# A fused attention and FFN kernel whose instructions the tile framework orders with its timeline model

## The chip, the cores and the metric

The kernel runs on one core of one Trainium2 chip. The metric is the device time of one execution in microseconds (us), as the median of three runs. Five engines work side by side, each through its own queue of instructions in order: TensorE (PE in the profile; its weight loads are PEld), VectorE (DVE), ScalarE (ACT), GpSimd (POOL) and SyncE (SP, which issues most of the DMA transfers).

## The reference

The reference has two parts. The first is linear attention with random features on q, k and v of 8 batches × 8 heads × 576 tokens × 64, with 128 features per head:

```python
def phi(x):
    proj = np.einsum('bhsd,md->bhsm', x, omega)
    sq = np.sum(x * x, axis=-1, keepdims=True) / 2.0
    h = proj - sq
    h = h - np.max(h, axis=-1, keepdims=True)
    return np.exp(h) / np.sqrt(m)
q_p, k_p = (phi(q_s), phi(k_s))
kv = np.einsum('bhsm,bhsd->bhmd', k_p, v)
z = np.sum(k_p, axis=2)
num = np.einsum('bhsm,bhmd->bhsd', q_p, kv)
den = np.einsum('bhsm,bhm->bhs', q_p, z)[..., None] + 1e-06
return (num / den).astype(np.float32)
```

The second takes that result as x, 4608 tokens of 512 values, through a bilinear FFN whose weights are given in float64 (`w1`, `w2` 512×1024, `w3` 1024×1024, `w_out` 1024×512):

```python
a = x @ w1
b = x @ w2
h = a * b @ w3
return (h @ w_out).astype(np.float32)
```

## The kernel before, in words

The 4608 tokens are 36 chunks of 128, batch after batch; a batch has four chunks and a half. Products are made from pairs of fp16 numbers: every operand is scaled by a power of two and split into a high and a low half, and each product is three matmuls (`PASSES`: high·high, high·low, low·high). The split is made by `split` (ACT or POOL writes the high half, L142 or L144; DVE the low half, L145).

**Weights.** The float64 words come in 20 blocks of 128×1024. `from_float64` (L462 to L494) has three steps for each: `fetch` issues the DMA on ACT's queue (L472), `magnitude` takes the absolute value of the high words on ACT (L480), and `bits` puts the float32 together with four instructions on DVE (L486, L488, L489, L490). `w1` and `w2` go to `w12b`, with sums of magnitudes for the scale (L510 on ACT, L514 on PE), and are split (`w12_split`). `w3` and `w_out` are multiplied once into one matrix: its row blocks are `wp_n` (L560, L562 on PE), which ACT copies to `Wb` (L574) and measures (L159); `W_split` splits them at the end.

**Chunks.** For a chunk of q or k, `norm` and `scale` find a scale from sums of squares, `split` makes `qhl` or `khl`, and `features` projects them on PE (L267, tiles `qpj`, `kpj`), takes the negated maximum on DVE (`nm`, L277), makes the exponential on ACT (L288, or with DVE's L290 first, L291), and splits it (`eq`, `ek`, L131, L133, L300). `kv_batch` forms a batch's `kv` (L348, `kvp`). `eq` is transposed by DMA (`eqT`), and `q_attend` multiplies it with `kv` (L384, `nu`), divides (`gd`, `gr`, `xs`, L394 to L400) and takes a maximum (L407). `x_turn` splits the result (`xhl`, L422 on ACT, L423 on DVE) and transposes it by DMA (`xT`, L427). `gate` makes both products with w1 and w2 (L622, `ab`), multiplies them (ACT L631, DVE L632, `asb`) and splits the result on POOL (L636, L637). `project_out` multiplies with the folded matrix (L651, `o`), scales on ACT (L655) and writes the chunk out. Names carry the chunk's number: `xhl_0` is chunk 0's, `ab_0_0` and `asb_0_0` are the gate of chunk 0, first half of the features. K runs ahead of q by five chunks, so that `kpj_6` goes with `qpj_1`.

**What sets the order.** The source issues the steps by a plan: `step` and `put` give each a tick and a rank, and a loop over the ticks calls them, with weight steps (`ORDER`, `PER`) and pieces of gate and projection between them. The recorded program then goes to the tile framework, which may reorder it: each engine's queue gets its final order from the framework's scheduler, with due regard to what depends on what; `tc.high_priority()` around a step (`x_turn` has it) gives its instructions precedence there. The framework also places the semaphores. Which scheduler is used is set where the context is opened, in `kernel()`, L847.

## Time and profile before

| what | value |
|---|---|
| time, median of three runs | 872.07 us (871.26 to 872.96) |
| profiled execution, first to last instruction | 870.8 us (the profile gives its time as this span alone) |
| mean granted TensorE clock | 0.957 |
| instructions | 20594 |
| busy: PE, DVE, ACT, POOL | 787.7, 614.1, 416.9, 305.4 us |
| moved by DMA | 88.43 MB, mean 102 GB/s |

Busy time is the union of an engine's instructions over the span. The page also cuts the span into 40 slices, 21.8 us each, with a digit for the busy tenths of each engine. A row of the timeline gives start, length, engine, line, operation and tiles, and in brackets the idle time just before with what ended it; a row of the groups gives the busy time of all such instructions in us, the mean of one in ns, and then the idle time before them. [...]

### The profile page before, as it was taken

To read this page: it belongs to the slowest core of one execution; us is meant where nothing else is said; L and a number is where in the kernel's file an instruction comes from. 1 tells how busy PE (TensorE), PEld (TensorE's weight loads), DVE (VectorE), ACT (ScalarE), POOL (GpSimd) and SP (SyncE) were. 2 spreads that over 40 slices of the span, in tenths; PEclk is the share of its full clock that TensorE was granted. 3 is DMA by queue.
4 is the path that set the end of the run, shared out by engine and by line. 5 is a ranking of instruction groups with operands and counts; after the bars stand their busy time and mean duration, and the time that the engine had idled before them with its cause. 6 is when DMAs were issued, how large, how long until landed. Compare 5 with 4: busy or idle time off the path is not lost.

```text
span 870.8 us, 20594 instructions
## 1 busy us (share of the span) xinstructions
PE 787.7 (90%) x8608; PEld 582.9 (67%) x8614; DVE 614.1 (71%) x1116; ACT 416.9 (48%) x748; POOL 305.4 (35%) x327
## 2 busy tenths in 40 slices
PE   0973499568997899999999999999999999999998
PEld 0432355466785777777777777777777767777774
DVE  5879888788868977776877777768777764563200
ACT  3588776777543743545355335453553342221111
POOL 0000003223253654444543544445435452233220
PEclk9985599779998999999999999999999999999999
DMA  8535557332334644434433453334342234332100
GB/s 307 189 109 195 151 150 219 102 82 39 88 96 110 122 89 124 81 87 86 122 98 86 95 125 77 84 86 122 101 90 67 62 78 72 72 62 49 31 19 36
DMA packets 142525, 88.43 MB, mean 102 GB/s; under 512 B 116704, under 2 KB 116832, under 8 KB 142432
## 3 DMA queue, kind: packets, MB, share of 16 engines
q1 hardware_dynamic: 134944, 66.15, 32.5%
q10 hardware_dynamic: 7488, 20.97, 7.1%
q8 instruction: 67, 1.10, 0.5%
q14 instruction: 26, 0.21, 0.1%
HBM read 49.35 MB, written 9.44 MB: 68 GB/s over the span
## 4 chain that ended last, share of the span: by engine, by line
PE 76%; DVE 10%; ACT 6%; DMA 4%; issue 3%; POOL 1%; ACTq 0%; SPq 0%; DVEq 0%; POOLq 0%
PE ab L622 40%; PE o L651 20%; PE kvp L348 3%; PE nu L384 3%; PE wp L562 3%; PE qpj L267 3%; PE kpj L267 2%; DVE nm L277 1%; DVE vhl L145 1%; ACT qe L288 1%; DMA qraw<-qT 1%; ACT ke L288 1%; DVE arena L489 1%; DMA arena<-wo 1%; DVE w12b L490 1%
## 5 line engine op out<-in xcount | busy, mean ns | idle before, releaser
L622 PE MATMUL ab<-xT,w12b 128*128 128x256 f16 (+1 forms) x3840 | 397.9, 264 | 8.4 <-DMA xT<-xhl 6.5
L622 PEld LDWEIGHTS <-w12b 128*128 128x128 f16 x3840 | 344.4, 99 | 50.3 <-issue 8.5
L651 PE MATMUL o<-Wb,arena 128*128 128x512 f16 x864 | 194.1, 379 | 2.2 <-DVE Wb L145 1.4
L651 PEld LDWEIGHTS <-arena 128*128 128x128 f16 x864 | 84.4, 100 | 95.1 <-issue 2.4
L636 POOL TENSOR_SCALAR arena<-asb 128x512 f16<-128x512 f32 x72 | 49.3, 685 | 217.9 <-DVE asb L632 207.3
L300 POOL TENSOR_TENSOR eq<-qe,eq 128x1024 f16<-128x1024 f32 x34 | 73.0, 2148 | 129.1 <-DVE eq L131 90.8
L291 ACT ACTIVATE qe<-qe,ln_e,es 128x1024 f32<-128x1024 f32 x31 | 38.4, 1239 | 112.3 <-DVE qe L290 112.3
L632 DVE TENSOR_TENSOR asb<-ab,asb 128x512 f32<-128x512 f32 x72 | 49.4, 686 | 59.1 <-PE ab L622 57.9
L300 POOL TENSOR_TENSOR ek<-ke,ek 128x1024 f16<-128x1024 f32 x28 | 59.7, 2132 | 88.9 <-ACT ek L133 44.7
L637 POOL TENSOR_TENSOR arena<-asb,arena 128x512 f16<-128x512 f32 x72 | 85.3, 1185 | 5.9
L291 ACT ACTIVATE ke<-ke,ln_e,es 128x1024 f32<-128x1024 f32 x27 | 33.5, 1241 | 79.0 <-DVE ke L290 62.4
L145 DVE SCALAR_TENSOR_TENSOR khl<-kraw,s,khl 128x512 f16<-128x512 f32 x36 | 53.9, 1497 | 16.2 <-ACT khl L142 16.2
L562 PE MATMUL wp<-w12b 128*128 128x512 f32 x128 | 59.0, 613 | 1.4 <-DVE w12b L490 1.4
L145 DVE SCALAR_TENSOR_TENSOR qhl<-qraw,s,qhl 128x512 f16<-128x512 f32 x36 | 32.1, 891 | 37.5 <-ACT qhl L142 37.5
L422 ACT ACTIVATE xhl<-xs,p2r 128x512 f16<-128x512 f32 x36 | 25.9, 719 | 58.1 <-DVE p2r L189 54.4
L631 ACT ACTIVATE asb<-ab 128x512 f32<-128x512 f32 x72 | 41.9, 582 | 24.6 <-PE ab L622 24.6
L267 PE MATMUL kpj<-om,khl 64*128 64x128 f16 x864 | 35.5, 231 | 17.0 <-ACT khl L142 11.5
L159 ACT ACTIVATE junk_q<-qraw 128x512 bf16<-128x512 f32 x36 | 22.7, 630 | 56.5 <-DMA qraw<-qT 56.5
L384 PEld LDWEIGHTS <-eqT 128*128 128x128 f16 (+1 forms) x960 | 32.6, 102 | 24.3 <-DMA eqT<-eq 13.6
L655 ACT ACTIVATE o<-o,oscs 128x512 f32<-128x512 f32 x36 | 24.2, 673 | 50.6 <-PE o L651 50.6
L384 PE MATMUL nu<-kv,eqT 128*128 128x65 f16 (+1 forms) x960 | 34.9, 196 | 13.6 <-DMA eqT<-eq 12.6
L131 DVE CAST eq<-qe 128x1024 f16<-128x1024 f32 x31 | 22.1, 713 | 35.3 <-ACT qe L291 35.3
(124 smaller groups left out, 1053.8 us busy)
## 6 DMA issues: line engine op xcount, KB each, us to landing
kraw<-kT SPq DMA_DIRECT2D x36, 256.0 KB, 2.8
vraw<-v SPq DMA_DIRECT2D x36, 256.0 KB, 3.0
qraw<-qT SPq DMA_DIRECT2D x36, 256.0 KB, 2.8
out<-o SPq DMA_DIRECT2D x36, 256.0 KB, 2.2
arena<-w3T ACTq DMA_DIRECT2D x8, 1024.0 KB, 5.8
arena<-w ACTq DMA_DIRECT2D x8, 1024.0 KB, 5.8
arena<-wo ACTq DMA_DIRECT2D x4, 1024.0 KB, 5.9
eqT<-eq SPq DMA_TRANSPOSE x72, 3.1
```

The lines of the kernel that those rows point to most:

```text
L145: nc.vector.scalar_tensor_tensor(lo, src, s, hi, ALU.mult, ALU.subtract)
L267: nc.tensor.matmul(pg[:, g, i], hl[d, x, i], om[d, y], start=first is None and n == 0, stop=n == len(PASSES) - 1,)
L291: nc.scalar.activation(e, e, AF.Exp, scale=es, bias=ln_e)
L300: (nc.vector if lo == "d" else nc.gpsimd).tensor_tensor(t[:, 1], e, t[:, 0], ALU.subtract)
L384: nc.tensor.matmul(nu[r0:r1, h // 4, h % 4], t[:, x, place(h), r0:r1], kvs[b][:, y, h], start=n == 0, stop=n == 2,)
L562: nc.tensor.matmul(ps, w[:, j, k * P : (k + 1) * P], guest[:, j], start=j == j0, stop=j == HALF - 1,)
L622: nc.tensor.matmul(ps[:, k], w12[m][i][cc][:, a, r * P : (r + 1) * P], x[:, b, cc, off : off + T], start=j == 0, stop=j == len(mm) - 1,)
L631: nc.scalar.mul(asb, ab[0], 2.0**-37)
L632: nc.vector.tensor_tensor(asb, ab[1], asb, ALU.mult)
L636: nc.gpsimd.tensor_scalar(h[:, 0], asb, 1.0, 1.0, ALU.mult, ALU.mult)
L637: nc.gpsimd.tensor_tensor(h[:, 1], asb, h[:, 0], ALU.subtract)
L651: nc.tensor.matmul(ps, hs[c, f][0][:, a], W[f][:, b], start=i == 0, stop=i == len(mm) - 1)
```

## The change

The tile context is opened with one more argument. The scheduler then chooses the order of the instructions with a timeline model of the machine instead of its default rule. Nothing that is computed changes; the matmuls, the passes of each engine and the DMA transfers are the same, in another order within each queue.

```diff
@@ -844,7 +844,7 @@
         for k, a in arrays.items()
     ]
     out = nc.dram_tensor("out", (B * S, arrays["wo"].shape[1]), F32, kind="ExternalOutput").ap()
-    with tile.TileContext(nc) as tc:
+    with tile.TileContext(nc, schedule_with_timeline_sim=True) as tc:
         weights = [a.bitcast(U32) for a in args[4:]]
         tile_favor_attention_then_bilinear_ffn(tc, *args[:4], *weights, out)
     r = run_bass_kernel_spmd(nc, [arrays], core_ids=[0])
```

Three places show what it moves. The numbers in the names below are the framework's own running numbers; what they stand for is said beside each.

DVE, around the low half of x for chunk 0 (`xhl_962` is `xhl_0`; `qhl_925` and `khl_930` are `qhl_1` and `khl_6`; `qpj_967` and `kpj_1010` are `qpj_1` and `kpj_6`). Before:

```order
L419 TENSOR_SCALAR pt_960<-p2p_4_956,pv 128x1
L423 SCALAR_TENSOR_TENSOR xhl_962<-xs_921,p2r_4_958,xhl_962 128x512
L486 TENSOR_SCALAR arena<-arena 128x1024
L145 SCALAR_TENSOR_TENSOR qhl_925<-qraw_496,s_4_880,qhl_925 128x512
L145 SCALAR_TENSOR_TENSOR khl_930<-kraw_528,s_4_880,khl_930 128x512
L488 TENSOR_SCALAR arena<-arena 128x1024
L489 SCALAR_TENSOR_TENSOR arena<-arena 128x1024
L490 SCALAR_TENSOR_TENSOR w12b<-arena 128x1024
L277 TENSOR_REDUCE nm<-qpj_967 128x8
L277 TENSOR_REDUCE nm<-kpj_1010 128x8
L286 TENSOR_SCALAR nm<-nm,es 128x8 x2
```

Now, in the same place:

```order
L394 TENSOR_SCALAR gd<-nu_892 128x8
L398 RECIPROCAL gr<-gd 128x8
L400 TENSOR_TENSOR xs_921<-nu_892,gr 128x512
L277 TENSOR_REDUCE nm<-qpj_967 128x8
L407 TENSOR_REDUCE mx<-xs_921 128x1
L286 TENSOR_SCALAR nm<-nm,es 128x8
L414 TENSOR_SCALAR mx<-mx 128x1
L277 TENSOR_REDUCE nm<-kpj_1010 128x8
L423 SCALAR_TENSOR_TENSOR xhl_962<-xs_921,p2r_4_958,xhl_962 128x512
L131 CAST ek_1047<-ke_1037 128x1024
L300 TENSOR_TENSOR eq_1004<-qe_994,eq_1004 128x1024
```

The two reductions with their two L286 now stand ahead of `xhl_962`, where they stood behind it, and so do the two splits and 18 instructions of weight blocks (five L486, five L488, five L489, three L490), further up in the queue: 24 instructions in all, and none went the other way.

PE, behind the gate matmuls of chunk 0 (`ab_0_1_1129`). `nu_1217` is `nu_1`, the attention product of chunk 1; `norm_q_k_1183` is the norm for q of chunk 2 and k of chunk 7; `wp_0_1199` and `wp_1_1205` are the seventh row block of the folded matrix, `wp_6`; `norm_v_1260` is the norm for v of batch 1. One piece of the difference, without the weight loads:

```order
+L164 MATMUL norm_q_k_1183<-sums_105,ones 128x3
+L560 MATMUL wp_0_1199<-Wb,ident 128x512
+L562 MATMUL wp_0_1199<-w12b 128x512 x4
+L560 MATMUL wp_1_1205<-Wb,ident 128x512
+L562 MATMUL wp_1_1205<-w12b 128x512 x4
 L384 MATMUL nu_1217<-kv_614,eqT_1007 128x65
-L164 MATMUL norm_q_k_1183<-sums_105,ones 128x3
-L560 MATMUL wp_0_1199<-Wb,ident 128x512
-L562 MATMUL wp_0_1199<-w12b 128x512 x4
-L560 MATMUL wp_1_1205<-Wb,ident 128x512
-L562 MATMUL wp_1_1205<-w12b 128x512 x4
 L164 MATMUL norm_v_1260<-vam_866,ones 128x8
```

The ten matmuls of `wp_6` and the norm stood behind the 24 of `nu_1` and now stand ahead of them.

ACT, around the cast of the features of q for chunk 2 (`eq_1341` is `eq_2`; `ke_1374` is k of chunk 7; `asb_0_1511` is the gate of chunk 1). Before:

```order
L288 ACTIVATE qe_1331<-qpj_1304,nm,es 128x128 x8
L288 ACTIVATE ke_1374<-kpj_1347,nm,es 128x128
L133 CAST eq_1341<-qe_1331 128x1024
L288 ACTIVATE ke_1374<-kpj_1347,nm,es 128x128 x7
L631 ACTIVATE asb_0_1511<-ab_0_0_1413 128x512
L133 CAST ek_1384<-ke_1374 128x1024
L510 ACTIVATE wab_2_1_1529<-w12b 128x1024
```

Now:

```order
L288 ACTIVATE qe_1331<-qpj_1304,nm,es 128x128 x8
L480 ACTIVATE arena<-arena 128x1024
L288 ACTIVATE ke_1374<-kpj_1347,nm,es 128x128 x8
L631 ACTIVATE asb_0_1511<-ab_0_0_1413 128x512
L510 ACTIVATE wab_2_1_1529<-w12b 128x1024
L133 CAST eq_1341<-qe_1331 128x1024
L133 CAST ek_1384<-ke_1374 128x1024
```

The cast of `eq_2` moved from behind one exponential of chunk 7 to behind all eight, a magnitude, the scaling of the gate and an L510.

On PE there are further swaps of this kind up to 227 us of the trace and between 268 and 302 us: among them `wp_4` and `wp_5` stand earlier, two matmuls of `nu_3` now stand ahead of `ab_2_0`, and 26 matmuls of `ab_4_2` ahead of `qpj_8`. On SP a few transfers of k change places with outputs.

## The prediction

> **What bounds the kernel now.** I read the page's busy times and its 40 slices first, since a change of order alone can only win or lose idle time.
>
> ```profile
> span 870.8 us, 20594 instructions
> PE 787.7 (90%) x8608; PEld 582.9 (67%) x8614; DVE 614.1 (71%) x1116; ACT 416.9 (48%) x748; POOL 305.4 (35%) x327
> PE   0973499568997899999999999999999999999998
> DVE  5879888788868977776877777768777764563200
> PEclk9985599779998999999999999999999999999999
> ```
>
> A slice is 21.8 us. From the fourteenth on PE stands at nine tenths; the open slices are all at the start, and there DVE is the densest engine and the granted TensorE clock falls to 0.5 and 0.7. The windows view (columns: stretch, length, busy of PE, PEld, DVE, ACT, POOL with their counts, granted clock, DMA share, GB/s) cuts that start where the orders of the two programs part and meet again.
>
> ```profile
> 0.00:20.00 20.00, 1.17 (x4) 1.00 (x4) 10.37 (x28) 6.20 (x10) 1.07 (x16) 1.00 0.90 331
> 20.00:114.00 94.00, 61.16 (x410) 34.23 (x413) 79.82 (x136) 68.59 (x138) 0.67 (x10) 0.75 0.50 160
> 114.00:136.00 22.00, 21.95 (x204) 13.77 (x203) 18.18 (x21) 18.12 (x44) 2.13 (x1) 1.00 0.65 157
> 136.00:156.00 20.00, 16.70 (x86) 7.98 (x85) 18.31 (x36) 10.54 (x22) 6.90 (x7) 1.00 0.68 210
> 156.00:189.00 33.00, 21.08 (x271) 18.84 (x274) 25.88 (x47) 27.25 (x59) 8.09 (x5) 0.69 0.37 89
> 189.00:227.00 38.00, 33.16 (x591) 27.14 (x593) 32.27 (x78) 26.96 (x55) 11.07 (x18) 1.00 0.25 60
> 227.00:270.00 43.00, 43.00 (x540) 33.05 (x535) 34.46 (x52) 16.40 (x25) 22.00 (x19) 1.00 0.37 97
> 270.00:302.00 32.00, 24.52 (x379) 19.73 (x378) 28.32 (x62) 21.41 (x37) 16.24 (x10) 0.89 0.54 108
> 302.00:870.00 568.00, 565.00 (x6139) 427.21 (x6137) 366.50 (x663) 221.43 (x365) 237.19 (x243) 1.00 0.36 81
> ```
>
> Three things follow. From 302 us on PE works 565.0 of 568 us at full clock: with the same matmuls behind it, the end of the program is the moment of 302 us plus 568. All that an order can change lies before that: PE idles there for (20 − 1.2) + (94 − 61.2) + 0.1 + (20 − 16.7) + (33 − 21.1) + (38 − 33.2) + 0 + (32 − 24.5) = 79 us. And from 20 to 227 us DVE is busy for 174.5 of 207 us, more than PE's 154.1: it converts the float64 weights (four instructions to a block, 20 blocks) and also makes each chunk's features, x and splits. So the order on DVE, and what it makes PE wait for, decides the start.
>
> **The change part by part.** Nothing is added or removed, so each cost is a position: how much work of an engine now stands ahead of an instruction on which another engine waits. Up to DVE's reduction `nm` of `qpj_5`, and on PE from the first `o_0` of the projection (both at 227 us of this trace), the two orders hold the same set of work ahead. So I follow one chain from the first place where it is late to 227 us, and add the difference to the end. Its stations before are these (DVE first, then PE; start and length in us).
>
> ```profile
> 113.60 0.75 DVE L423 SCALAR_TENSOR_TENSOR xhl<-xs,p2r,xhl 128x512 f16<-128x512 f32 x1 [0.68 <-ACT xhl L422]
> 115.25 0.75 DVE L145 SCALAR_TENSOR_TENSOR qhl<-qraw,s,qhl 128x512 f16<-128x512 f32 x1
> 115.92 0.75 DVE L145 SCALAR_TENSOR_TENSOR khl<-kraw,s,khl 128x512 f16<-128x512 f32 x1
> 147.68 4.03 DVE L145 SCALAR_TENSOR_TENSOR vhl<-vraw,s,vhl 128x512 f16<-128x512 f32 x4 [0.59 <-POOL vhl L144]
> 154.21 2.35 DVE L490 SCALAR_TENSOR_TENSOR w12b<-arena 128x1024 uint32<-128x1024 uint32 x2
> 156.48 1.22 DVE L277 TENSOR_REDUCE nm<-qpj 128x8 f32<-128x1024 f32 x1
> 177.48 0.75 DVE L423 SCALAR_TENSOR_TENSOR xhl<-xs,p2r,xhl 128x512 f16<-128x512 f32 x1 [0.21 <-ACT xhl L422]
> 188.83 0.69 DVE L632 TENSOR_TENSOR asb<-ab,asb 128x512 f32<-128x512 f32 x1 [0.46 <-PE ab L622]
> 226.95 1.23 DVE L277 TENSOR_REDUCE nm<-qpj 128x8 f32<-128x1024 f32 x1
> ```
>
> ```profile
> 127.30 5.52 PE L622 MATMUL ab<-xT,w12b 128*128 128x128 f16 x96
> 132.66 0.90 PE L384 MATMUL nu<-kv,eqT 128*128 128x65 f16 x24
> 133.61 1.11 PE L560 MATMUL wp<-Wb,ident 128*128 128x512 f32 x2
> 142.28 0.28 PE L164 MATMUL norm_v<-vam,ones 128*128 128x8 f32 x2
> 157.00 7.15 PE L622 MATMUL ab<-xT,w12b 128*128 128x128 f16 x96
> 181.40 7.32 PE L622 MATMUL ab<-xT,w12b 128*128 128x128 f16 x96 [5.83 <-DMA xT<-xhl]
> 275.17 0.39 PE L267 MATMUL qpj<-om,qhl 64*128 64x128 f16 x4 [4.86 <-ACT qhl L142]
> ```
>
> *First term, `xhl_0`.* The order on DVE now has 24 more instructions ahead of `xhl_0` and none fewer: five L486, five L488, five L489 and three L490 of weight blocks, the reductions of `qpj_1` and `kpj_6` with their two small L286, and the splits `qhl_1`, `khl_6`. The groups view gives what one takes (last figures of the first part: total us, mean ns).
>
> ```profile
> L489 DVE SCALAR_TENSOR_TENSOR arena<-arena 128x1024 uint32<-128x1024 uint32 x20 | 24.5, 1224 | 0.4
> L490 DVE SCALAR_TENSOR_TENSOR w12b<-arena 128x1024 uint32<-128x1024 uint32 x20 | 24.4, 1222 | 1.8 <-PE wp L562 1.5
> L486 DVE TENSOR_SCALAR arena<-arena 128x1024 f32<-128x1024 f32 x20 | 15.0, 751 | 4.9 <-ACT arena L480 4.7
> L488 DVE TENSOR_SCALAR arena<-arena 128x1024 uint32<-128x1024 uint32 x20 | 13.8, 689 | 0.3
> L277 DVE TENSOR_REDUCE nm<-qpj 128x8 f32<-128x1024 f32 x36 | 43.8, 1216 | 2.2 <-PE qpj L267 2.0
> L286 DVE TENSOR_SCALAR nm<-nm,es 128x8 f32<-128x8 f32 x14 | 3.1, 226 | 0.1
> xT<-xhl SPq DMA_TRANSPOSE x36, 3.1
> ```
>
> 5 × 0.751 + 5 × 0.689 + 5 × 1.224 + 3 × 1.222 + 2 × 1.217 + 2 × 0.226 + 2 × 0.75 = 21.4 us. Neighbours overlap a little (the split at 115.25 ends after the next begins at 115.92), so I take 0.06 off each: 20.0. If these instructions fell into time in which DVE now idles, less would be left. From 20 to 114 us it idles 94 − 79.8 = 14.2 us, gaps between 136 instructions among them; the durations of all that stands ahead of `xhl_0` sum to 98.2 us, 15.4 less than its start, and 20 − 10.4 = 9.6 of these lie before 20 us, so some 6 us are plain waiting. So the bounds are +6 (all of the 14.2 filled) and +21.4, and I take +20, near the upper end, because what was moved ahead waits for the same transfers and matmuls as before. `xhl_0` then starts at 133.6.
>
> *Second term, PE and `nu_1`.* From the start of `xhl_2` (177.48) to the matmuls that need its transpose (181.40) it was 3.9 us, of which the transfer is 3.1. So `ab_0_0` begins at 137.5, instead of 127.30. In the trace it had not waited: PE was full from 114 to 136 us. Part of what filled it (the products `wp_4`, `wp_5`, the projections of chunk 1) now lies earlier, so PE has nothing ahead of `ab_0_0` to do and idles for some 10 us. Behind it stand, new, the ten matmuls of `wp_6` ahead of `nu_1`: before they came after it. They took 142.28 − 133.61 = 8.7 us. `nu_1` therefore ends at 137.5 + 5.5 + 0.2 + 8.7 + 0.9 = 152.8. After such an idle stretch `ab` may take what it took at 157.00 and 181.40, 7.15 and 7.32 us in a window with clock 0.69, instead of 5.52 at clock 1.00: then 154.5. [...]
>
> *Third term, what waits for `nu_1`.* DVE's `gd` of chunk 1 heads a queue. Behind it, to the reduction of `qpj_2`, stand its own short steps with two 0.69 us passes over x (2.4 in all), the scale of v (0.9), the five splits of v (4.03 + 0.8), `xhl_1` (0.75) and two L490 (2.35): 11.2 us of work, of which before the change most came ahead of that reduction without a wait. It lands at 152.8 + 0.2 + 11.2 = 164.2, or 165.9 with a cold clock, against 156.48: +7.7 to +9.4. From below: if DVE did not idle at all between 114 us and here, the 11.2 us would hide the wait and the station came at +4.
>
> *Fourth term, chunk 2.* From that reduction to `xhl_2` it was 21.0 us, with 18.2 us of DVE work between; in the new order 25.3 us of work stand there, since two blocks of L486 to L490 and the first w12 splits moved ahead of it. Also ACT casts `eq_2` later; in the trace it stood between the exponentials of chunk 7.
>
> ```profile
> 161.23 1.03 ACT L133 CAST eq<-qe 128x1024 f16<-128x1024 f32 x1
> 162.16 2.55 ACT L288 ACTIVATE ke<-kpj,nm,es 128x128 f32<-128x128 f32 x7
> 295.10 1.25 PE L622 MATMUL ab<-xT,w12b 128*128 128x256 f16 x10 [0.67 <-DMA xT<-xhl]
> ```
>
> Now these seven (2.55), a magnitude, the scaling of `ab_1_0` and an L510 (three passes, some 1 us each like the cast) come first, and the start of the row is held 1.5 to 2 us by the reduction of `kpj_7`: about 7 us in all. `nu_2`, which ended 13 us after the reduction before, then ends some 20.5 after it; DVE's own work reaches `gd` of chunk 2 after 19.6. So `xhl_2` starts 25.3 to 26.7 us behind the reduction, and the product `asb_2_0` follows 11.35 us later as before (188.83 − 177.48): 36.7 to 38.0 us, against 188.83 − 156.48 = 32.35. That adds 4.3 to 5.7. Sum: 7.7 + 4.3 = +12.0 to 9.4 + 5.7 = +15.1; I take +13.5, the middle, for neither the clock nor the cast decides alone.
>
> *Fifth term, to 227 us.* From `asb_2_0` to the reduction of `qpj_5` it was 38.1 us, filled on DVE to 32.3 of 38 and on PE to 33.2. Both orders have the same work there, so the lateness is handed on: 0. What could be won is the 5 us that both leave open; I leave it for the lower bound.
>
> *Sixth term, 270 to 302 us.* PE waited 4.86 us at 275.17 for the split of q for chunk 8, with `ab` matmuls that needed nothing queued behind it. Now 26 matmuls of `ab_4_2` stand ahead of it (at 0.12 to 0.2 us some 4 us): up to −4.9. Against it, `xhl_7` stands behind 8.1 us more of DVE work and could hold up `ab_6`, which the trace has waiting only 0.67 us for its transpose; up to +3. I take 0. [...]
>
> *Sum.* Span 870.8 + 13.5 = 884.3. The median of the three runs, 872.07, lies 1.3 above the profiled span (time around it and between runs), so 885.6 on the runs' scale, say **885.5 us**.
>
> **The rivals.** *A, the packing is better.* The blocks of bits come 8 to 16 us of DVE work earlier, and so do the products that PE makes of them. If what I call delay only fills idle time, then `nm` of `qpj_2` comes at +4, the 64.3 us of DVE work from there to 227 us runs without a gap (160.6 + 64.3 = 224.9, that is −2), and the stalls of 270 to 302 us close (−7.5): 872 − 9.5, about 862. For it: DVE leaves 32 us of 207 open, PE 79 of 302. Against it: the gate is `xhl_0`, then `nu_1`, and both are later by work that one can count. *B, no change.* At 227 us the work is the same, so a chain not limited by `xhl_0` or `nu_1` would be absorbed: 872. For it: PE is full from 227 us and would hide anything that ends by then. Against it: PE idled only 4.8 us in the 38 before, too little to take back 13. *C, more stalls.* Two matmuls of `nu_3` now stand ahead of `ab_2_0`, and they need the transposes of `eq_3`, which I reckon to be there 2 us before `xT`. If ACT is a few us later with that cast, PE stands still with `ab_2_0`, and with it DVE's queue behind `asb_2_0`: +4 there, on top of the upper ends +15.1 and +3 of the sixth term, 872 + 22 = 894; with a second such wait for chunk 3, 900.
>
> **How the numbers follow.** The likeliest case, with its own range 879 to 890 (the terms at +7 to +18), gets 0.57; C gets 0.20, A 0.16, B 0.07. Two runs of this kernel differ by up to 0.2% (871.26 to 872.96), which is what a measurement can tell from no change. So faster 0.16, same 0.07, slower 0.77. The range runs from 868, which leaves out most of A, to 897, which holds the larger part of C.
>
> **What would show it.** Right: `xhl_0` near 134 us and `ab_0_0` behind a wait of several us for `xT`; DVE waiting near 147 to 153 us for `nu` by PE; `nm` of `qpj_2` near 165, `asb_2_0` near 202, the reduction of `qpj_5` near 240; after that PE as full as before, with 565 us for the rest. Wrong: `xhl_0` before 125 us (the early blocks filled idle time), a PE that is as full between 114 and 156 us as it was, or an end that moves less than the station at 227 us does, which would mean that PE still had slack behind it.

## The result and the profile after

The changed kernel takes 882.59 us (median of four runs, 881.76 to 883.40), the kernel before 872.52 us in the same comparison (871.26 to 873.62): a ratio of 1.0114, with a 95% interval of 1.0100 to 1.0128, or 10 us more. The forecast was 885.5 us and slower. The profiled execution of the changed kernel has a span of 881.6 us, 10.8 more than before.

The same stretches of the windows view as in the prediction, now of the changed kernel (columns as there):

```profile
0.00:20.00 20.00, 3.22 (x30) 2.62 (x30) 12.71 (x34) 7.30 (x12) 1.13 (x16) 1.00 0.93 343
20.00:114.00 94.00, 68.02 (x391) 33.35 (x388) 88.45 (x141) 80.71 (x162) 0.79 (x10) 0.85 0.61 206
114.00:136.00 22.00, 13.04 (x171) 12.24 (x172) 10.58 (x17) 8.58 (x20) 2.12 (x1) 0.56 0.22 42
136.00:156.00 20.00, 19.74 (x114) 9.72 (x115) 13.15 (x29) 8.71 (x18) 7.01 (x7) 1.00 0.32 94
156.00:189.00 33.00, 12.14 (x180) 9.86 (x182) 26.88 (x46) 26.76 (x58) 6.92 (x4) 0.72 0.38 95
302.00:870.00 568.00, 565.93 (x6265) 432.21 (x6266) 346.19 (x681) 225.27 (x367) 238.28 (x245) 1.00 0.36 82
```

From 20 to 114 us DVE works 88.45 us instead of 79.82, and before 20 us 12.71 instead of 10.37: the early weight blocks filled gaps. Between 114 and 136 us PE does 13.0 us of work instead of 21.95, since part of it is done already, and then it catches up. The open place is 156 to 189 us: 12.1 us of PE work instead of 21.1. After 302 us PE is as full as before.

The stations of the chain, from the timeline of DVE in the changed kernel (start, length; the low half of x for chunk 0, `gd` of chunk 1, the reduction of `qpj_2`, the low half of x for chunk 2, `asb_2_0`, the reduction of `qpj_5`):

```profile
123.77 0.75 DVE L423 SCALAR_TENSOR_TENSOR xhl<-xs,p2r,xhl 128x512 f16<-128x512 f32 x1 [1.69 <-ACT xhl L422]
...
145.44 0.17 DVE L394 TENSOR_SCALAR gd<-nu 128x8 f32<-128x8 f32 x1 [5.68 <-PE nu L384]
...
156.33 1.21 DVE L277 TENSOR_REDUCE nm<-qpj 128x8 f32<-128x1024 f32 x1
...
183.52 1.84 DVE L423 SCALAR_TENSOR_TENSOR xhl<-xs,p2r,xhl 128x512 f16<-128x512 f32 x1
...
197.16 0.69 DVE L632 TENSOR_TENSOR asb<-ab,asb 128x512 f32<-128x512 f32 x1 [7.92 <-PE ab L622]
...
233.27 1.23 DVE L277 TENSOR_REDUCE nm<-qpj 128x8 f32<-128x1024 f32 x1 [0.25 <-PE qpj L267]
```

And from the timeline of PE (`ab_0_0`, `nu_1`, then chunk 2: two pieces of `nu_2`, two matmuls of `nu_3`, `ab_2_0`; last, `nu_8`, `kvp_2` and `ab_6_0`):

```profile
127.64 8.17 PE L622 MATMUL ab<-xT,w12b 128*128 128x128 f16 x96 [7.85 <-DMA xT<-xhl]
...
144.50 0.90 PE L384 MATMUL nu<-kv,eqT 128*128 128x65 f16 x24
...
156.85 5.52 PE L622 MATMUL ab<-xT,w12b 128*128 128x128 f16 x96
...
167.71 0.59 PE L514 MATMUL l<-wab,ones_bf 128*128 128x512 bf16 x1 [5.16 <-ACT wab L510]
171.72 0.29 PE L384 MATMUL nu<-kv,eqT 128*128 128x65 f16 x2 [3.42 <-DMA eqT<-eq]
...
175.57 1.42 PE L384 MATMUL nu<-kv,eqT 128*128 128x65 f16 x22
...
185.76 0.29 PE L384 MATMUL nu<-kv,eqT 128*128 128x65 f16 x2 [5.35 <-DMA eqT<-eq]
188.70 8.35 PE L622 MATMUL ab<-xT,w12b 128*128 128x128 f16 x96 [2.65 <-DMA xT<-xhl]
...
302.61 1.48 PE L384 MATMUL nu<-kv,eqT 128*128 128x65 f16 x24 [4.62 <-DVE p2p L186]
304.38 5.11 PE L348 MATMUL kvp<-vhl,ek 128*128 128x65 f16 x120 [0.29 <-DVE ke L290]
...
311.10 5.07 PE L622 MATMUL ab<-xT,w12b 128*128 128x256 f16 x45 [1.17 <-DMA xT<-xhl]
```

Put beside the rows of before, in us:

| station | before | after | later by | forecast |
|---|---|---|---|---|
| `xhl_0` on DVE | 113.60 | 123.77 | 10.2 | 20.0 |
| `ab_0_0` on PE | 127.30 | 127.64 | 0.3 | 10.2 |
| end of `nu_1` | 133.56 | 145.40 | 11.8 | 19.2 to 20.9 |
| reduction of `qpj_2` | 156.48 | 156.33 | −0.2 | 7.7 to 9.4 |
| `xhl_2` | 177.48 | 183.52 | 6.0 | |
| `asb_2_0` | 188.83 | 197.16 | 8.3 | 12.0 to 15.1 |
| reduction of `qpj_5` | 226.95 | 233.27 | 6.3 | 13.5 |
| end of the span | 870.8 | 881.6 | 10.8 | 13.5 |

So, in these two traces, the place of the first forecast delay costs nothing in the end. The time is lost between the reductions of `qpj_2` and `qpj_5` (6.5 us), and again behind the second (4.5 us).

### The profile page after: what moved, and what is told of

Read it like the earlier page. It is cut to its first block, busy times and chain, and to the rows that moved or that the text cites. A ratio compares the mean times of both kernels' runs of the same rounds, so it can differ in the third digit from the quotient of the medians.

```text
span 881.6 us, 20589 instructions
## 1 busy us (share of the span) xinstructions
PE 790.6 (90%) x8610; PEld 584.3 (66%) x8614; DVE 587.4 (67%) x1116; ACT 419.6 (48%) x748; POOL 302.8 (34%) x327
## 4 chain that ended last, share of the span: by engine, by line
PE 70%; DVE 4%; ACT 2%; DMA 2%; issue 1%; POOL 0%; ACTq 0%; DVEq 0%
PE ab L622 40%; PE o L651 21%; PE nu L384 3%; PE qpj L267 2%; PE kvp L348 2%; PE kpj L267 2%; DMA qraw<-qT 1%; PE norm_q_k L164 1%; DMA xT<-xhl 1%; DVE nm L277 1%; DVE vhl L145 1%; ACT ke L291 1%; ACT qe L288 0%; DVE xhl L423 0%; DVE qhl L145 0%
## 5 line engine op out<-in xcount | busy, mean ns | idle before, releaser
L300 POOL TENSOR_TENSOR eq<-qe,eq 128x1024 f16<-128x1024 f32 x34 | 72.3, 2128 | 97.6 <-DVE eq L131 81.6
L300 POOL TENSOR_TENSOR ek<-ke,ek 128x1024 f16<-128x1024 f32 x28 | 59.6, 2129 | 96.5 <-ACT ek L133 60.5
L423 DVE SCALAR_TENSOR_TENSOR xhl<-xs,p2r,xhl 128x512 f16<-128x512 f32 x36 | 30.2, 840 | 48.2 <-ACT xhl L422 48.0
L145 DVE SCALAR_TENSOR_TENSOR qhl<-qraw,s,qhl 128x512 f16<-128x512 f32 x36 | 34.8, 967 | 38.2 <-ACT qhl L142 38.2
L562 PEld LDWEIGHTS wp<-w12b 128*128 128x128 f32 x128 | 25.0, 199 | 30.6 <-issue 29.8
L267 PE MATMUL kpj<-om,khl 64*128 64x128 f16 x864 | 35.2, 230 | 11.2 <-ACT khl L142 4.4
```

The source lines that it names most:

```text
L145: nc.vector.scalar_tensor_tensor(lo, src, s, hi, ALU.mult, ALU.subtract)
L267: nc.tensor.matmul(pg[:, g, i], hl[d, x, i], om[d, y], start=first is None and n == 0, stop=n == len(PASSES) - 1,)
L300: (nc.vector if lo == "d" else nc.gpsimd).tensor_tensor(t[:, 1], e, t[:, 0], ALU.subtract)
L562: nc.tensor.matmul(ps, w[:, j, k * P : (k + 1) * P], guest[:, j], start=j == j0, stop=j == HALF - 1,)
```

## Experiments

All twelve kernels compute the same instructions. Their queues are written out: a table holds the order of each engine, and an issue-order edge, which needs no semaphore (by which one engine waits for another's work, or for a transfer), ties each instruction to the one ahead of it.

```python
for queue in steps:
    names = [f"I-{n}" for n in itertools.accumulate(queue)]
    for a, b in zip(names, names[1:]):
        tc.add_manual_dep(here[b], a, info, reason="pinned order")
```

Thus the two orders can be spliced, or one instruction moved, with all others held. `s1_head_sems`, `best_try` and the runs whose names begin with `m_` have their semaphores from the timeline scheduler, the others from the default one. Two places are good for splicing, because the two orders have the same set of instructions ahead of them on every engine: one behind `wp_6` on PE and at the reduction of `qpj_2` on DVE (some 156 us), and one at the first 24 matmuls of `qpj_5` and `kpj_10` on PE and the reduction of `qpj_5` on DVE (some 227 us).

**Control and three stretches.** The first run has the order before throughout; the other three have the new order in one stretch alone.

```diff
 stretch     to 156 us   to 227 us   rest
 before      before      before      before
-changed     new         new         new
+s1_head     new         before      before
+s2_middle   before      new         before
+s3_tail     before      before      new
```

> Control: the queues of the kernel before, written out as a table and held by issue-order edges that need no semaphore. Every instruction stands where it stood. Theory and rivals alike: the same time as before, within 0.2% (870.8 to 874.3 us). If it differs, the pinning itself has a price, and the other spliced orders must be read against this run.

> Only the first stretch of the new order (on every engine up to the reduction of qpj_2, some 156 us of either trace), then the order before. The prediction's second and third terms (xhl_0 late, wp_6 ahead of nu_1) say that this stretch costs +7.7 to +9.4 us: 880 to 882. The rival, from the two traces, in which that reduction starts at 156.48 and at 156.33 us: the lateness is all absorbed by then, 0, at most -1.6 because the gate of chunk 1 then runs warm: 871 to 873.

> Only the second stretch of the new order (from the reduction of qpj_2 to that of qpj_5, some 156 to 227 us), the order before ahead of it and behind it. The prediction's fourth and fifth terms say +4.3 to +5.7: 877 to 878. The rival, from the traces: it is the whole of what is late at the reduction of qpj_5, +6.3 (226.95 against 233.27): 878.8, and if what 197 to 233 us gave back belongs to the first stretch, +8.3: 881.

> Only the third stretch of the new order (behind the reduction of qpj_5). The prediction's sixth term says 0 (between -4.9 and +3): 872.5. The rival, from the traces: PE stands 4.62 us before nu_8, with no matmul of ab_4_3 left to fill the wait, and the end is 4.5 us later relative to that reduction: 877. A third possibility: this loss only arises because the middle is late, then 872.5 or less, with the 4.86 us stall of qpj_8 shortened by 2 to 3: 870.

Measured: the control 872.59 us, a ratio to before of 1.0004 (0.9995 to 1.0013), so that the table has no price of its own. `s1_head` 875.09 us, 1.0036 (1.0023 to 1.0050): between the theories, neither. `s2_middle` 881.31, 1.0103 (1.0089 to 1.0117): not the 877 to 878 of the prediction's terms, but the larger of the two figures that the traces gave. `s3_tail` 876.34, 1.0047 (1.0034 to 1.0059), as the traces said and not 0.

The surprise of `s1_head` has its cause in the first microseconds. The timeline of ACT, first of the changed kernel:

```profile
0.74 0.94 ACTq L472 DMA_DIRECT2D arena<-wo  x2
1.71 0.49 ACTq L472 DMA_DIRECT2D arena<-w3T  x1
...
5.91 1.12 ACT L480 ACTIVATE arena<-arena 128x1024 f32<-128x1024 f32 x1 [2.39 <-DMA arena<-wo]
```

and then of `s1_head`, whose queues are the same there:

```profile
0.74 0.94 ACTq L472 DMA_DIRECT2D arena<-wo  x2
9.45 0.37 ACTq L472 DMA_DIRECT2D arena<-w3T  x1
9.85 1.28 ACT L480 ACT_TABLE_LOAD   x1 [9.85 <-DMA kraw<-kT]
11.15 1.12 ACT L480 ACTIVATE arena<-arena 128x1024 f32<-128x1024 f32 x1
```

The third transfer stands at the same place of the queue, but waits until 9.45 us for a transfer of k. That is no dependency of the data: the built program has a wait there for the semaphore that a load of k raises, which the changed kernel has not. Which semaphore a transfer gets is settled by the scheduler, and not by the order of the queues alone. So the same table was built once more with the semaphores of the timeline scheduler.

```diff
-    with tile.TileContext(nc) as tc:
+    with tile.TileContext(nc, schedule_with_timeline_sim=True) as tc:
```

> The same queues as the first-stretch run (the new order up to the reduction of qpj_2, then the order before), but its semaphores given out by the timeline scheduler, as in the changed kernel. In the first-stretch run ACT's third transfer (w3T) was issued at 9.45 us behind a wait for a transfer of k, in the changed kernel at 1.71 without one, and DVE's first conversion started at 12.30 against 7.06. Theory: that wait alone made the 2.7 us, so this run comes at 871 (870.5 to 872.5), the reduction of qpj_2 again near 156.3. Rival: the splice itself costs, then 875 as before.

Measured: 871.88 us, a ratio of 0.9996 (0.9987 to 1.0005), no difference from before. On ACT the third transfer is issued at 1.71 us again, and on DVE the reduction of `qpj_2` starts at 155.05 us:

```profile
1.71 0.49 ACTq L472 DMA_DIRECT2D arena<-w3T  x1
```

```profile
155.05 1.21 DVE L277 TENSOR_REDUCE nm<-qpj 128x8 f32<-128x1024 f32 x1
```

So the first stretch of the new order costs nothing, although `xhl_0` and `nu_1` are some 10 us late in it. A station of one trace is only good to a microsecond or two. Over all the runs of this section, that reduction starts at 156.21 to 157.75 us in the five traces with the order before up to there, and at 154.45 to 156.33 in the eight with the new order and its semaphores. If anything, the new head is about 1 us early.

The three stretches sum to −0.04 + 1.03 + 0.47 = 1.46% against 1.14% of the whole. The difference, 2.8 us, is little more than the four intervals together allow (some 2 us). Of it 1.7 us can be seen in the middle, where the reduction of `qpj_5` is 8.0 us late in `s2_middle` (234.99) and 6.3 in the changed kernel. The changed kernel comes into that stretch with a faster gate of chunk 1 (5.52 us at 156.85 against 7.62 at 157.63 in `s2_middle`); that this is the reason isn't shown, and neither is what the default scheduler's semaphores do in `s2_middle` and `s3_tail`.

**What holds chunk 2.** The next runs start from the changed kernel and move single steps of the middle stretch back. First the cast that the prediction's fourth term named (ACT; on POOL the low half of `eq_2` likewise):

```diff
 L288 ACTIVATE qe_1331<-qpj_1304,nm,es 128x128 x8
+L133 CAST eq_1341<-qe_1331 128x1024
 L480 ACTIVATE arena<-arena 128x1024
 L288 ACTIVATE ke_1374<-kpj_1347,nm,es 128x128 x8
 L631 ACTIVATE asb_0_1511<-ab_0_0_1413 128x512
 L510 ACTIVATE wab_2_1_1529<-w12b 128x1024
-L133 CAST eq_1341<-qe_1331 128x1024
 L133 CAST ek_1384<-ke_1374 128x1024
```

> The changed kernel's queues with one thing moved: on ACT the cast of eq_2 from behind a magnitude, the eight exponentials of chunk 7, asb_1_0 and an L510 to right behind its own exponentials, and on POOL the low half of eq_2 ahead of the split of asb_1_0. Theory 1 (the late cast is the loss of the middle stretch): the transposes of eq_2 land some 5 us earlier, nu_2, xhl_2 and ab_2_0 follow, 877 to 878. Theory 2 (three queues hold chunk 2, each in its place): the 22 matmuls of nu_2 stand behind those of qpj_3, which wait for DVE's split qhl_3 (171.93 us), and gd of chunk 2 stands behind the reduction of qpj_3 on DVE; 882 to 883, no gain above 1 us.

Measured: 881.73 us, 1.0109 (1.0095 to 1.0122), no gain that can be told. The late cast alone isn't the loss.

Next, `nu_2` on PE ahead of `qpj_3`, and the steps of chunk 2 on DVE and ACT ahead of what had overtaken them; without and with the two matmuls of `nu_3` put back.

```diff
 PE
 nu_2 x2
+nu_2 x22
 qpj_3 x24
 l1_1_1 x2
-nu_2 x22
 kpj_8 x24
-nu_3 x2                                (m_chain_nu3 only)
 ab_2_0 x96
 norm, l1_1_1 x2
+nu_3 x2                                (m_chain_nu3 only)
 nu_3 x22
 DVE
+gd, gr, xs, mx, mx, p2p, p2r, pt of chunk 2
 w12 split, nm and L286 of qpj_3
+xhl_2
 w12 split
-gd, gr, xs, mx, mx, p2p, p2r, pt of chunk 2
 w12 split, nm of kpj_8
-xhl_2
 ACT
+xhl_2 (L422)
 w12 split, w12 split, qe_3 x8, w12 split, cast of eq_3
-xhl_2 (L422)
```

> As m_cast, and nu_2 in one piece ahead of qpj_3 on PE, the eight steps of chunk 2 from gd to pt ahead of the first w12 split and the reduction of qpj_3 on DVE, xhl_2 ahead of two w12 splits and a reduction on DVE, and ahead of two w12 splits, the exponentials and the cast of chunk 3 on ACT. The two matmuls of nu_3 stay ahead of ab_2_0. Theory 2: xhl_2 starts near 179 instead of 183.5 and its transpose lands near 183, but the two matmuls of nu_3 wait for the transpose of eq_3 until about 186, so ab_2_0 begins there instead of at 188.7: 2.7 us won, 880. Theory 1: the same as m_cast. Rival (nu_3 costs nothing): 5 to 6 us won, 877.

> As m_chain, and the two matmuls of nu_3 moved behind ab_2_0 to the other 22. Theory 2: ab_2_0 begins when xT lands, near 183, 5.5 us won in all, 877. If it equals m_chain, the two matmuls of nu_3 cost nothing. If neither gains, the lateness of chunk 2 is not what makes the middle stretch longer.

Measured: 882.95 us, 1.0122 (1.0108 to 1.0135), and 883.87 us, 1.0129 (1.0111 to 1.0147). Both missed: no gain at all. By what was written beforehand, the lateness of chunk 2 would then not be the loss; but chunk 2 was still late, for `ab_2_0` began at 189.54 us, 0.8 later than in the changed kernel. The timelines of `m_chain_nu3` say why. DVE, PE and SP:

```profile
180.22 0.75 DVE L423 SCALAR_TENSOR_TENSOR xhl<-xs,p2r,xhl 128x512 f16<-128x512 f32 x1
```

```profile
189.54 7.76 PE L622 MATMUL ab<-xT,w12b 128*128 128x128 f16 x96 [12.49 <-DMA xT<-xhl]
```

```profile
184.90 1.24 SPq L371 DMA_TRANSPOSE eqT<-eq  x1
186.27 1.26 SPq L427 DMA_TRANSPOSE xT<-xhl  x1
187.64 1.28 SPq L371 DMA_TRANSPOSE eqT<-eq  x1
```

`xhl_2` is ready at 181 us, but its transpose is issued at 186.27, behind a transpose of `eq_3`, which waits until 184.90 for the cast of chunk 3. The new order had changed places of transposes on SP too; the list under "The change" names only transfers of k and outputs there. In the changed kernel it isn't seen as a wait, because `xhl_2` is late there itself (its transpose was issued at 185.40, as it ended). So the fourth queue:

```diff
 L215 DMA kraw_1576<-kT 128x512
-L371 DMA_TRANSPOSE eqT_1657<-eq_1654 128x8x128
 L427 DMA_TRANSPOSE xT_1615<-xhl_1612 128x8x128
-L371 DMA_TRANSPOSE eqT_1657<-eq_1654 128x8x128
+L371 DMA_TRANSPOSE eqT_1657<-eq_1654 128x8x128 x2
 L215 DMA qraw_1874<-qT 128x512
```

> As m_chain_nu3, and on SP's queue the transpose of xhl_2 moved ahead of the first transpose of eq_3, where it stood before the change. In m_chain_nu3 xhl_2 started at 180.22 us, but ab_2_0 only at 189.54 behind 12.49 us of waiting for xT, 9.3 us later, where it is 3.9 elsewhere. Theory 3 (SP's queue is the fourth that holds chunk 2: xT waits in it behind a transpose of eq_3, which needs the cast of chunk 3): ab_2_0 begins near 184, 5 us earlier, and the end follows: 878 to 879. Rival (the middle stretch ends by something else, the products of w12 for the second half or Wb): ab_2_0 earlier, the end not: 882 to 884.

Measured: 878.15 us, 1.0065 (1.0052 to 1.0079), as theory 3 said. On PE and SP of this run:

```profile
182.68 8.32 PE L622 MATMUL ab<-xT,w12b 128*128 128x128 f16 x96 [7.34 <-DMA xT<-xhl]
```

```profile
179.58 1.35 SPq L427 DMA_TRANSPOSE xT<-xhl  x1
183.44 3.44 SPq L371 DMA_TRANSPOSE eqT<-eq  x2
```

`ab_2_0` begins 6.9 us earlier than in `m_chain_nu3`, and the reduction of `qpj_5` starts at 227.34 us, 0.4 behind the kernel before. Part of that is the early head of this trace (the reduction of `qpj_2` at 154.62): from the one reduction to the other it takes 72.7 us, against 77.4 in `m_chain_nu3`, 76.9 in the changed kernel and 70.5 before. So most of the loss of the middle is undone, 5.7 us of the time, when the fourth edit joins the first three, which by themselves gained nothing. That SP's order alone would do it isn't shown (in the changed kernel the transpose was issued as `xhl_2` ended, so that `xhl_2` itself came too late), nor which of the other three it needs.

**The third stretch.** There PE's new order takes `ab_4_2` ahead of `qpj_8` and uses up `ab_4_3` early.

```diff
 PE, behind nu_6
-ab_4_2_0 x5
+ab_4_2_0 x20, ab_4_2_1 x6
 qpj_8 x4
 ...
-nu_7 x24, ab_4_2_1 x12
-ab_4_3_0 x9, qpj_9 x24, ab_4_3_0 x5, kpj_14 x4, ab_4_3_0 x3, kpj_14 x20, ab_4_3_0 x7, ab_4_3_1 x24
-nu_8 x24, ab_6_0_0 x10, kvp_2 x120
+ab_4_2_1 x12
+ab_4_3_0 x24, ab_4_3_1 x9, nu_7 x24, ab_4_3_1 x15, qpj_9 x24, kpj_14 x24
+nu_8 x24, kvp_2 x120, qpj_10 x12, ab_6_0_0 x24
```

> The queues before, with PE alone in the new order behind the reduction of qpj_5: 26 matmuls of ab_4_2 ahead of qpj_8, all of ab_4_3 ahead of qpj_9, none of ab_6_0 ahead of kvp_2. Theory (in the third stretch the loss is that PE has used up its filling matmuls when it waits for the transposes of eq_8): the +4.0 of the third-stretch run return, 876 to 877. Rival (DVE's and SP's orders make it, by taking xhl_7 behind 8 us more of work): PE alone costs less than 1, or gains up to 2.6 at qpj_8: 870 to 873.

Measured: 877.41 us, 1.0051 (1.0039 to 1.0064). PE's order alone costs what the whole stretch costs (1.0047). It shortens the wait for `qpj_8` and makes longer ones behind it, where no `ab` is left. PE of `t_pe_only`:

```profile
276.14 0.39 PE L267 MATMUL qpj<-om,qhl 64*128 64x128 f16 x4 [1.89 <-ACT qhl L142]
...
295.81 1.48 PE L384 MATMUL nu<-kv,eqT 128*128 128x65 f16 x24 [3.06 <-DVE qe L290]
298.85 5.86 PE L348 MATMUL kvp<-vhl,ek 128*128 128x65 f16 x120 [1.57 <-DVE ke L290]
```

Before, `qpj_8` waited 4.86 us and `nu_8` not at all for data that the view names.

A mixture of the best stretches was to beat both kernels:

```diff
 new order to the reduction of qpj_2, the order before behind it, and on PE
+ab_4_2_0 x14
 qpj_8 x4
-ab_4_2_0 x5
 kpj_13 x4
-ab_4_2_0 x9
```

> A mixture meant to be faster than both: the new order up to the reduction of qpj_2 with the timeline scheduler's semaphores (871.9 by itself), the order before behind it, and 14 matmuls of ab_4_2 moved ahead of the first of qpj_8, where PE stood 4.86 us. These take about 2 us at the start of the wait. If the wait was free time, 870; if they are missing as filling behind qpj_8 and kpj_13, as in the third stretch of the new order, 872 or more.

Measured: 871.76 us, 0.9994 (0.9985 to 1.0003): the same as before. The wait of `qpj_8` shrank from 4.86 to 3.35 us, and new waits of 0.33, 0.76 and 0.54 us came behind it.

The last run joins the two repairs, to see whether the account closes.

```diff
 m_all
-PE behind the reduction of qpj_5: new order
+PE behind the reduction of qpj_5: order before   (DVE, ACT, POOL, SP keep the new one)
```

> As m_all, and PE's queue behind the reduction of qpj_5 in the order before (the other engines keep the new order there). In m_all that reduction starts at 227.34 us, 0.4 behind the kernel before, and the span is 875.9, so what is left is the third stretch. Theory (PE's order there is the whole of it, +4.5 in the run of PE alone): 873.4 to 874.2, within 0.2% of before. Rival (the other engines' new order there costs by itself, xhl_7 behind 8 us more of DVE's work above all): 876 or more.

Measured: 895.96 us, 1.0261 (1.0247 to 1.0275). The theory missed by 22 us. The rival's "or more" holds the time, but not by the step it named. DVE and PE of this run:

```profile
292.54 0.69 DVE L632 TENSOR_TENSOR asb<-ab,asb 128x512 f32<-128x512 f32 x1 [3.35 <-PE ab L622]
...
302.46 0.69 DVE L632 TENSOR_TENSOR asb<-ab,asb 128x512 f32<-128x512 f32 x1 [5.13 <-PE ab L622]
303.07 0.68 DVE L407 TENSOR_REDUCE mx<-xs 128x1 f32<-128x512 f32 x1
```

```profile
308.89 1.48 PE L384 MATMUL nu<-kv,eqT 128*128 128x65 f16 x24 [6.53 <-DVE p2p L186]
317.45 2.29 PE L622 MATMUL ab<-xT,w12b 128*128 128x256 f16 x10 [7.09 <-DMA xT<-xhl]
```

DVE's new queue has the products `asb_4_2` and `asb_4_3` early, as PE's new order delivers them. With PE's old order they come late, DVE stands before them, and what is queued behind them (`mx`, the features, `xhl` of the next chunks) is what PE then waits for. So PE's new order can't be taken back alone: alone it costs 4.9 us, and alone in the new surroundings its absence costs 18. What the third stretch would take with all queues put right is known only from the order before itself. One engine's new order alone in the middle stretch wasn't run. With PE's, DVE's or ACT's the queues would there wait for each other in a circle; SP's alone is possible, and what it costs by itself stays open.

## Why the prediction was right, and where it was not

The direction and the range held, and the time is 2.9 us from the forecast. The mechanism held only in part: the delay of 7.7 to 9.4 us at the head, more than half of the forecast, didn't come, and two later terms that were too small happened to make up for it. That the sum is so near is luck. One of the prediction's own signs of being wrong came true (`xhl_0` at 123.77, before 125 us), and the reduction of `qpj_2`, `asb_2_0` and the reduction of `qpj_5` came 8.7, 4.8 and 6.7 us before the times named as signs of being right. The wait of `ab_0_0` for `xT` and the full PE after 302 us were as foreseen.

*First term, `xhl_0`: too large.* The 24 instructions were costed at 20 us; `xhl_0` came 10.2 us later. The bounds were +6 and +21.4, and the choice within them failed: "near the upper end, because what was moved ahead waits for the same transfers and matmuls as before". Their work was there, but DVE's gaps from 20 to 114 us took in 8.6 us of it (88.45 − 79.82), and those before 20 us another 2.3 (12.71 − 10.37).

*Second term: the mechanism right, the size off by the first.* `ab_0_0` waits for `xT` now (7.85 us), `wp_6` stands ahead of `nu_1` for 8.7 us (135.84 to 144.50), and the gate took 8.17 us, over which the granted clock was 0.66 (forecast 7.15 to 7.32 us; before, 5.52 at 1.00). So 2.65 us were lost with the lower clock, more than the 1.6 to 1.8 by the rows of before (7.15 and 7.32 less 5.52). This loss varies: the same matmuls took 7.25 us behind a wait of 8.48 in `s1_head_sems`. By what rule the clock falls and rises no run here shows. But `ab_0_0` began 0.3 us later and not 10.2. Before, `xhl_0` plus the 3.9 us of its transpose would have allowed 117.5; PE came to it at 127.30. This slack of 9.8 us was in the rows quoted, and takes up the 10.2.

*Third term: the queue behind `gd` right, its start not.* From `gd` to the reduction of `qpj_2` it took 156.33 − 145.44 = 10.9 us, forecast 11.2. But since `nu_1` ended at 145.40 and not at 152.8, the reduction is not late at all. `s1_head_sems` shows it: 0.9996.

*Fourth term: right place, too small.* 197.16 − 156.33 = 40.8 us against 32.35, so +8.5, forecast +4.3 to +5.7. `xhl_2` came 27.2 us behind the reduction (forecast 25.3 to 26.7). From it to `asb_2_0` it took 13.6 us where the forecast kept the 11.35: `xhl_2` took 1.84 us instead of 0.75, and `ab_2_0` took 8.35 us at a granted clock of 0.64 instead of 7.32 at 0.74. The cast, the place of `nu_2` and DVE's queue were all named, but only as alternatives of which the slower decides. The runs fit holds in series instead: with ACT's, PE's and DVE's put back nothing was gained, with SP's as well 5.7 us. SP's the prediction left out: its rule that each cost is a position in a queue was not applied to the transpose of `xhl_2`.

*Fifth term:* forecast 0, measured 36.1 us against 38.1, −2.0.

*Sixth term: the sign wrong.* Taken as 0 within −4.9 and +3; it was +4.5. The gain was there (the wait of `qpj_8` is 2.2 us instead of 4.86), but the filling matmuls that made it were missing where `nu_8` waits, 4.62 us. `s3_tail` (1.0047) and `t_pe_only` (1.0051) bear it out.

So −0.2 + 8.5 − 2.0 + 4.5 = 10.8 us of span: the delay at the head fell away and the fifth term gave back (10.7 us less than forecast), and two terms were too small (8.0 us). Rival A had the packing of DVE right, not its worth: the filled gaps made the new head free, not faster than before. Rival B, that lateness is absorbed, holds for the head alone. Of rival C, the place (chunk 2, `nu_3` ahead of `ab_2_0`) was a true wait (5.35 us), but moving `nu_3` back gained nothing as long as the transpose was held on SP.

## What to carry to other kernels

An order of instructions is one thing over all queues: a place that is late may be free as long as slack stands behind it (here `xhl_0` and `nu_1`, some 10 us late at a ratio of 0.9996), and a single row put back gains nothing while a second or a fourth queue, the DMA issues included, holds the same step (here 881.73 us with the cast put back, 883.87 with three queues, 878.15 with SP's as well). For each step that a scheduler has moved, follow the producer and the consumer through every queue to the next point at which both orders have done the same work, and compare the times there. And a wait filled with ready work isn't won until one has looked where that work was missing next (here the wait of `qpj_8` fell from 4.86 us to 2.2, and `nu_8` waited 4.62).

## What the runs showed that had not been expected

The semaphore that a transfer gets can delay it as an order can: here the third transfer on ACT was issued at 9.45 us instead of 1.71. In `s1_head` and `s1_head_sems` the queues are the same, and the wait of one transfer for another's semaphore, which moved the first conversion on DVE from 7.06 us (in the changed kernel) to 12.30 us, goes with 875.09 against 871.88 us. That no other of the reassigned semaphores has a part in it was not tried by itself.

DVE's busy time fell by 26.7 us, from 614.1 to 587.4, with the same instructions, and the kernel became slower. The group that shows it, of before and then of after (total us, mean ns):

```profile
L145 DVE SCALAR_TENSOR_TENSOR khl<-kraw,s,khl 128x512 f16<-128x512 f32 x36 | 53.9, 1497 | 16.2 <-ACT khl L142 16.2
```

```profile
L145 DVE SCALAR_TENSOR_TENSOR khl<-kraw,s,khl 128x512 f16<-128x512 f32 x36 | 27.6, 769 | 0.9 <-ACT khl L142 0.9
```

In the steady part of before, such a split lies beside POOL's L300 and takes 2.10 us, as here (DVE, then POOL):

```profile
514.08 2.10 DVE L145 SCALAR_TENSOR_TENSOR khl<-kraw,s,khl 128x512 f16<-128x512 f32 x1 [0.81 <-ACT khl L142]
```

```profile
513.50 2.13 POOL L300 TENSOR_TENSOR ek<-ke,ek 128x1024 f16<-128x1024 f32 x1 [1.92 <-ACT ek L133]
```

The split began while POOL's pass ran and ended 0.55 us after it, as if it had waited for it. Before, 20 of this group's 36 splits took 2.1 us, and every one of them began some 0.58 us into such a pass; of the 16 that took 0.75 none began within a pass of POOL. In the new order the split comes ahead of that pass and takes 0.75 (changed kernel, DVE, then POOL):

```profile
522.67 0.75 DVE L145 SCALAR_TENSOR_TENSOR khl<-kraw,s,khl 128x512 f16<-128x512 f32 x1
```

```profile
523.59 2.13 POOL L300 TENSOR_TENSOR ek<-ke,ek 128x1024 f16<-128x1024 f32 x1 [2.53 <-ACT ek L133]
```

So a beginning within such a pass goes with 2.1 us instead of 0.75 in these rows; that the pass is the cause isn't shown, since no run here takes it away. PE is full in that part (565.0 and 565.9 of 568 us), so these microseconds are worth nothing to the end.
